# A fused linear-attention and FFN kernel: other warm-up matmuls, other release points for its first loads, and another model of the DMA in its planner

## The chip, the cores and the metric

The kernel runs on one core of one Trainium2 chip. A core has a matrix engine (PE in the profile; its weight loads are shown as PEld), a vector engine (DVE), a scalar engine (ACT), GpSimd (POOL) and a queue engine (SP), each with its own in-order list of instructions; they meet through semaphores. Sixteen DMA engines move data between device memory (HBM) and the on-chip memory. PE writes to eight accumulation banks, which DVE and ACT read.

The metric is the device time of one execution in microseconds. Before the change the median of seven runs is 193.08 us (191.82 to 193.83).

## The reference

```
# q, k, v, f_logit: [4, 8, 768, 48]; moe_w_gate, moe_w_val: [384, 1536]; moe_w_out: [1536, 384]
f = 1 / (1 + exp(-f_logit))
for t in range(768):
    state = f[:, :, t, :, None] * state + outer(k[:, :, t], v[:, :, t])      # per batch and head, 48 x 48
    y[:, :, t] = q[:, :, t] @ state
x = y with heads side by side                                                # [3072, 384]
out = (relu(x @ w_gate) * (x @ w_val)) @ w_out                               # [3072, 384], float32
```

## The kernel before

The sequence is cut into six chunks of 128 tokens. For each chunk c the four batches are taken as two pairs, written c.0 and c.1 in the load order. The recurrence is computed chunk by chunk: cumulative sums of log-forgets by a matmul (L594), exponentials on ACT (L608), q and k scaled by them ("hats", L610), transposes (L642), scores (L667), a mask (L683 on DVE; two of them per pair in chunk 0 by ACT and POOL, L678 and L680), the outputs y (L712, L717) copied to xT (L729), and the state (L692, L564, L568, L570). Chunks 0 and 1 take this form (`attention_pair`); later chunks have a similar one.

The FFN of a chunk follows: twelve steps j of 128 hidden columns. A step has a gate group and a val group of three matmuls each (L922), a relu on ACT (L928) and a product on DVE (L932). Then the output projection (L965) with w_out, a copy (L975) and a store (L979). All FFN groups are chained in the order in which the code creates them (`chain("ffn", ...)`), so a group whose weights are missing holds up every later one. `halves` says, for chunks 0 to 2, how many of the first steps j are done for pair 0 alone and then for pair 1 alone, with 256 columns, before the rest is done for both with 512.

Each of the three weight matrices is loaded in thirds of four steps, cast to bf16 on the way: wg0, wg1, wg2 of w_gate, wv0 to wv2 of w_val, wo0 to wo2 of w_out. POOL issues them (L508), in the order wg0, wv0, wg1, wv1, wg2, wv2, wo0, wo1, wo2. SP issues the loads of f, k, q and v (L487), a whole pair at a time, 384 KB each. The string `first` lists the first loads; `x@y` means that the issuing engine waits for y to have landed before it issues x. The wait stands in the engine's own list, so all that is behind it there waits too: on POOL the elementwise work, on SP the later loads. Later loads of SP wait for a load three places earlier.

The order on every engine comes from a planner (`Plan`): a list scheduler with a fixed duration for each operation takes at each step the operation that can start first, by priority among equals. Its `transfers` works out when each load lands, packet by packet, with the two queues (SP's and POOL's) taking turns; `settle` alternates the two eight times. Only the order that comes out reaches the program, not the planned times.

At the start PE has nothing to do for some microseconds, and fillers are put in: matmuls of zeros into the last bank, whose result nobody reads. The kernel before puts them ahead of any operation planned to start by 15 us: as many matmuls of 512 columns (L1024) as fill 0.6 or 0.9 of the planned gap, after one at the very start (L1015). The zeros are set by DVE (L415).

The prediction speaks of f0.1 (the load of f for pair 1 of chunk 0), v0.0, k0.1, v0.1, q0.1 (named alike), of wg0, wv0, wg1, wv1, and of f1.0, k1.0, q1.0, v1.0, k1.1, wo0 and wo1.

Of the kernel before, what the change touches and what calls it, by code (L numbers as in the profile page):

```python
# [8 lines left out]
BF16 = mybir.dt.bfloat16  # L9
# [33 lines left out]
class Plan:  # L43
# [10 lines left out]
    def add(self, eng, emit, reads=(), writes=(), occ=0.5, lat=0.2, prio=0, opens=(), after=(), follows=()):  # L54
        op = Op(eng, emit, list(reads), list(writes), occ, lat, prio, opens, after, follows)
        op.idx = len(self.ops)
        self.ops.append(op)
        return op
# [128 lines left out]
    def transfers(self):  # L187

        rings = {e: [op for op in self.order[e] if op.parts] for e in ("SP", "POOL")}
        todo, at = {e: [] for e in rings}, {e: 0 for e in rings}  # L190
        issue = {"SP": 0.0}
        held = {e: [] for e in rings}
        sent, owed, t, last = 0, 0, 0.0, None
        pending = None
        sp = rings["SP"]
        queue = {e: [] for e in rings}
        for op in rings["POOL"]:
            queue["POOL"].append([op, op.parts[0], op.start + op.parts[3]])
        nxt = 0

        def feed():
            nonlocal nxt, pending, owed
            while True:
                if pending is not None:
                    if owed - sent > self.depth:
                        return
                    pending.issued = max(t, issue["SP"])
                    issue["SP"] = pending.issued
                    pending = None
                if nxt == len(sp):  # L210
# [12 lines left out]
        while True:  # L223
            feed()
            heads = {e: queue[e][0] for e in queue if queue[e]}
            if not heads:
                break
            can = {e: h for e, h in heads.items() if h[2] <= t}
            if not can:
                times = [h[2] for h in heads.values()]  # L230
                if nxt < len(sp) and pending is None:
                    times.append(max(sp[nxt].ready, issue["SP"]))
                t = max(t + 0.01, min(times))
                continue
            e = next(iter(can)) if len(can) == 1 else ("POOL" if last == "SP" else "SP")
            h = can[e]
            t += h[0].parts[1 if len(can) == 1 else 2] / 1000.0
            last = e
            h[1] -= 1
            if e == "SP":  # L240
                sent += 1
            if h[1] == 0:
                h[0].land = t + (self.tail[0] if e == "POOL" else 0.65 if t < 14.0 else self.tail[1])
                queue[e].pop(0)

    def settle(self, banks, rounds, early):
        self.depth, self.lag, self.tail = 250, 2.4, (1.6, 2.6)
        for i in range(rounds):
            self.schedule(banks)
            if i < rounds - 1:  # L250
                self.transfers()
                for op in self.ops:
                    if op not in early:
                        op.land = op.issued = None
        return self.order
# [47 lines left out]
def bass_hgrn2_outer__then__ffn_reglu_kernel(  # L303
# [10 lines left out]
    twos = (0, 1)  # L314
    pe_hats = {(0, 0), (0, 1), (1, 0), (1, 1)}
    by_pool = {(0, 0, 0, 1), (0, 1, 0, 1)}
    halves = {0: 6, 1: 4, 2: 6}
    x_way = {(c, pr): "tiled" if c < 5 else "xbar" for c in range(6) for pr in range(2)}
    s_twin = {(c, pr) for c in range(6) for pr in range(2)}
    y_twin = {(c, pr) for c in range(2, 5) for pr in range(2)}  # L320
# [1 line left out]
    act_copies, dve_q, single = set(), set(), set()  # L322
    flight = 3
    wsteps = 3
    first = ("f0.0 k0.0 q0.0 v0.0 f0.1 k0.1 v0.1 wg0@f0.1 wv0 wg1 wv1 q0.1 wg2@wv0 wv2 f1.0@wv1 k1.0 q1.0 v1.0 wo0@q1.0 wo1 "
             "k1.1 f1.1 q1.1 v1.1@f1.1 wo2").split()
    B, H, S, D = q.shape
    C = 128
    NC = S // C
# [11 lines left out]
    sb = nc.alloc_sbuf_tensor  # L341
# [40 lines left out]
    mask2 = sb("mask2", [128, 2, 2, 64], BF16)  # L382
    ident = sb("ident", [128, 128], BF16)
    ones = sb("ones", [128, 1], BF16)
    zeros = sb("zeros", [128, 512], BF16)
    banks = [nc.alloc_psum_tensor(f"ps{i}", [128, 512], F32) for i in range(8)]

    pl = Plan({"bc": 2, "bc4": 4, "tp": 2, "s": 4, "y": 2, "kv": 2, "f": 4})
    add = pl.add
    gp, ve, sc, te, sy = nc.gpsimd, nc.vector, nc.scalar, nc.tensor, nc.sync  # L390
# [13 lines left out]
    def pool_t(n):  # L404
        return dict(occ=0.1 + n * 2.2 / 1000.0, lat=0.12)
# [7 lines left out]
    def fill(eng, name, ap, value, cols, prio, key=None):  # L413
        e = engine[eng]
        add(eng, lambda: e.memset(ap, value), [], [key or name], occ=0.07 + cols / (1090.0 if eng == "DVE" else 1020.0), prio=prio)  # L415
# [19 lines left out]
    for t, name, src, sname in ((upto, "upto", tri, "tri"), (below, "below", tris, "tris")):  # L435
        add("DVE", lambda t=t, src=src: ve.tensor_tensor(t[:], src[:], same.ap[:, 0:128], ALU.mult), [same, sname], [name],
            occ=0.25, prio=-19)
    add("DVE", lambda: ve.tensor_copy(pick2[:], same.ap[:, 0:128].rearrange("p (b t) -> p b t", b=2)[:, :, 0]), [same], ["pick2"],
        occ=0.1, prio=-19)
    for i, src, name in ((0, upto, "upto"), (1, below, "below"), (1, upto, "upto")):  # L440
# [3 lines left out]
            src[:, 64:128].unsqueeze(1).to_broadcast([128, len(lo), 64]), ALU.add), [name], [f"mask2_{i}{m}" for m in lo],  # L444
            prio=-9, **pool_t(64 * len(lo)))

    fill("DVE", "zeros", zeros[:], 0.0, 256, -30)
    for i in range(NB):
        fill("DVE", f"bneg{i}", bneg[:, i], 0.0, 512, -28 if i < 1 else 11 if i < 2 else 30)
    for i in range(NH):  # L450
# [47 lines left out]
    def load_w(nm, s, after):  # L498
        if nm == "wo":
            src = bass.AP(tensor=w_out.tensor, offset=s * WJ * 128 * DM,  # L500
                          ap=[[DM, 128], [128 * DM, WJ], [1, DM]])
            dst = wo[:, s * WJ:(s + 1) * WJ, :]
        else:
            src = bass.AP(tensor=wsrc[nm].tensor, offset=s * WJ * 128,
                          ap=[[DFF, 128], [128 * DFF, NK], [1, WJ * 128]])
            dst = (wg if nm == "wg" else wv)[:, :, s * WJ * 128:(s + 1) * WJ * 128]
        last = tails.get("load_w")
        op = add("POOL", lambda: gp.dma_start(dst, src), [], [f"{nm}{s}"], occ=0.8, lat=1.2, prio=50, after=after,  # L508
                 follows=[last] if last else [])
        tails["load_w"] = op  # L510
        dma(op, f"{nm}{s}", 2.45, (32, 62, 80, 2.2) if nm == "wo" else (24, 80, 80, 2.6))
        return op

    loads, done, firsts = [], {}, []
    for item in first:
        item, _, behind = item.partition("@")
        gate = [done[behind]] if behind else []
        if item[0] == "w":
            op = load_w(item[:2], int(item[2:]), gate)
        else:  # L520
            c, b = int(item[1]), int(item[3])
            b0, b1 = (2 * b, 2 * b + 2) if item[2] == "." else (b, b + 1)
            op = load(item[0], c, b0, b1, gate)
# [485 lines left out]
    for item in pend[:-1]:  # L1009
        ffn_out(*item)  # L1010
    ffn_end(NC - 1, B - 1, [(0, 256), (256, DM)])

    WARM = 512
    warm_until = 15.0
    add("PE", lambda: te.matmul(banks[-1][:, 0:WARM], zeros[:, 0:128], zeros[:, 0:WARM]), ["zeros"], ["warm"], occ=0.2,  # L1015
        prio=-30)
    for e in pl.ENGINES:
        pl.free0[e] = 0.8
    spare = banks[-1]
    order = pl.settle([(bk, warm_until if bk is spare else 0.0) for bk in banks], rounds=8, early=set(firsts))  # L1020
    waits = pl.needs()

    def warm():
        return te.matmul(spare[:, 0:WARM], zeros[:, 0:128], zeros[:, 0:WARM], start=True, stop=True, skip_group_check=True)  # L1024

    busy, at, begun = [], pl.free0["PE"], False
    for op in order["PE"]:
        gap, each = op.start - at, 0.44 if at < 4.0 else 0.23
        if begun and op.start <= warm_until:
            for _ in range(int((0.9 if gap > 1.5 else 0.6) * gap / each)):  # L1030
                busy.append((op, warm))
        begun = True
        at = op.start + op.occ
    fillers = {}
    for op, emit in busy:
# [2 lines left out]
    for e in ("PE", "ACT", "DVE", "POOL"):  # L1038
        n = 0
# [75 lines left out]
```

## Time and profile before

| | us |
|---|---|
| median of seven runs (lowest, highest) | 193.08 (191.82, 193.83) |
| the profiled execution | 191.82 |
| its span, first to last instruction of the program | 190.1 |
| PE busy | 181.1 |
| ACT busy | 109.8 |
| DVE busy | 104.8 |
| POOL busy | 75.6 |

Times in the views are microseconds from the start of the span. A timeline row gives start, duration, engine, line, operation, output and inputs, and how many instructions it merges; in brackets stands the idle time ahead of it and what ended that. "POOLq" and "SPq" are the parts of these engines that issue; a DMA row there is the issue of a transfer, not the transfer. The chain of work that ended last is followed back from the last instruction; a DMA in it runs from its issue to its landing, and "issue" is time for which the profile shows no reason.

In the profiled execution f, k, q and v of pair 0 are issued from 0.81 to 2.97 us and those of pair 1 from 4.17 to 7.75. The first weight is issued at 9.41, and the load of f1.0 at 22.13.

### The profile page before, as it was taken

What the parts mean: (1) busy time and instruction counts of PE and PEld (TensorE: products, weight loads), DVE (VectorE), ACT (ScalarE), POOL (GpSimd) and SP (SyncE); (2) the same over time, 40 slices, a digit from 0 to 9 for tenths busy, and PEclk for the clock granted to TensorE, in tenths of its full rate; (3) what the DMA queues carried; (4) which work ended last, traced back from release to release, by engine and by line L of the source; (5) the groups of instructions that cost most, each with busy time, mean ns of one, the idle gap of its engine ahead of it and who ended that gap; (6) DMA issues with size and microseconds to landing.
All of it is one profiled execution on the core that took longest, in us unless ns stands there. A gap on an engine that the chain in (4) does not pass through costs nothing.

```text
span 190.1 us, 5012 instructions
## 1 busy us (share of the span) xinstructions
PE 181.1 (95%) x2061; PEld 107.9 (57%) x2079; DVE 104.8 (55%) x189; ACT 109.8 (58%) x244; POOL 75.6 (40%) x109
## 2 busy tenths in 40 slices
PE   7888799999999999999999999999999999999994
PEld 2456584566685466768545564554555555554564
DVE  7799364994555866518696375625538233343300
ACT  3774459835598486575867739476533533334322
POOL 8497404752376638446375473806300000000000
PEclk9999999999999999999999999999999999999999
DMA  6999999998999999999999999999640310011113
GB/s 158 325 273 204 174 246 282 214 233 166 254 210 211 209 165 211 219 224 222 147 209 196 179 216 213 231 213 226 129 100 19 86 41 32 9 45 41 41 53 112
DMA packets 108854, 32.04 MB, mean 169 GB/s; under 512 B 101792, under 2 KB 108832, under 8 KB 108832
## 3 DMA queue, kind: packets, MB, share of 16 engines
q1 hardware_dynamic: 104848, 28.19, 70.6%
q0 software_dynamic: 3984, 3.54, 11.9%
q8 instruction: 16, 0.26, 0.6%
q14 instruction: 6, 0.05, 0.1%
HBM read 25.95 MB, written 4.72 MB: 161 GB/s over the span
## 4 chain that ended last, share of the span: by engine, by line
PE 82%; DMA 11%; POOL 3%; issue 2%; SPq 1%; ACT 0%; POOLq 0%
PE ps L922 47%; PE ps L965 23%; DMA wo<-in_moe_w_out_dram 4%; DMA wv<-in_moe_w_val_dram 4%; PE ps L852 3%; DMA q_in<-in_q_dram 2%; PE ps L817 2%; POOL hats L610 2%; PE ps L751 1%; PE ps L900 1%; POOL vpad L657 1%; PE ps L945 1%; PE ps L712 1%; SPq L487 1%; PE ps L754 0%
## 5 line engine op out<-in xcount | busy, mean ns | idle before, releaser
L932 DVE TENSOR_TENSOR gT<-relu,ps 128x512 bf16<-128x512 bf16 (+1 forms) x88 | 51.0, 588 | 61.3 <-PE ps L922 38.5
L928 ACT ACTIVATE relu<-ps 128x512 bf16<-128x512 f32 (+1 forms) x88 | 45.6, 522 | 27.9 <-PE ps L922 26.8
L922 PE MATMUL ps<-xT,wv 128*128 128x512 bf16 (+1 forms) x262 | 60.7, 340 | 0.6 <-DMA wv<-in_moe_w_val_dram 0.3
L922 PE MATMUL ps<-xT,wg 128*128 128x512 bf16 (+1 forms) x249 | 57.9, 338 | 0.7 <-issue 0.2
L965 PE MATMUL ps<-wo,gT 128*128 128x384 bf16 x276 | 49.1, 326 | 0.4 <-DMA wo<-in_moe_w_out_dram 0.4
L965 PEld LDWEIGHTS ps<-wo,gT 128*128 128x128 bf16 x276 | 26.2, 98 | 18.7 <-DMA wo<-in_moe_w_out_dram 1.0
L922 PEld LDWEIGHTS ps<-xT,wv 128*128 128x128 bf16 x264 | 25.0, 98 | 19.5 <-DMA wv<-in_moe_w_val_dram 0.4
L922 PEld LDWEIGHTS ps<-xT,wg 128*128 128x128 bf16 x264 | 24.8, 98 | 19.8 <-issue 1.7
L975 ACT ACTIVATE osb<-ps 128x384 f32<-128x384 f32 x23 | 11.2, 494 | 26.5 <-PE ps L965 26.4
L773 POOL TENSOR_TENSOR hats<-k_in,expo 128x384 bf16<-128x384 f32 x16 | 15.8, 998 | 19.0 <-ACT expo L761 15.4
L827 DVE TENSOR_TENSOR ptm<-ps,tri 128x512 bf16<-128x512 f32 x32 | 20.4, 683 | 5.3 <-PE ps L817 5.2
L570 POOL TENSOR_TENSOR st<-ssum,dec 128x384 bf16<-128x384 f32 x16 | 13.1, 832 | 19.9 <-DVE ssum L568 19.9
L777 POOL TENSOR_TENSOR hats<-q_in,expo 128x384 bf16<-128x384 f32 x16 | 15.7, 1000 | 3.7 <-DMA q_in<-in_q_dram 3.7
L568 DVE TENSOR_TENSOR ssum<-ps,st 128x384 f32<-128x384 f32 x16 | 8.4, 552 | 3.7 <-PE ps L900 3.5
L683 DVE TENSOR_TENSOR ptm<-ps,mask 128x512 bf16<-128x512 f32 x14 | 8.7, 680 | 1.7 <-PE ps L667 1.7
L761 ACT ACTIVATE expo<-ps 128x384 f32<-128x384 f32 x16 | 7.9, 491 | 2.8 <-PE ps L754 2.7
L763 ACT ACTIVATE expo<-ps 128x384 f32<-128x384 f32 x16 | 8.0, 500 | 0.0
L807 POOL CAST vpad<-v_in 128x384 bf16<-128x384 f32 x16 | 7.7, 509 | 0.6 <-DMA v_in<-in_v_dram 0.6
L729 ACT ACTIVATE xT<-ps 128x384 bf16<-128x384 f32 x8 | 4.2, 597 | 5.5 <-PE ps L717 5.4
L742 ACT ACTIVATE f_in<-f_in 128x768 f32<-128x768 f32 x8 | 6.7, 842 | 0.8 <-DMA f_in<-in_f_logit_dram 0.8
L744 ACT ACTIVATE bneg<-f_in 128x768 bf16<-128x768 f32 x8 | 6.8, 845 | 0.1
L881 ACT ACTIVATE xT<-ps 128x384 bf16<-128x384 f32 x12 | 5.2, 486 | 2.6 <-PE ps L852 2.6
(85 smaller groups left out, 161.1 us busy)
## 6 DMA issues: line engine op xcount, KB each, us to landing
f_in<-in_f_logit_dram SPq DMA_DIRECT2D x12, 384.0 KB, 5.7
k_in<-in_k_dram SPq DMA_DIRECT2D x12, 384.0 KB, 5.6
q_in<-in_q_dram SPq DMA_DIRECT2D x12, 384.0 KB, 4.9
v_in<-in_v_dram SPq DMA_DIRECT2D x12, 384.0 KB, 5.3
out_dram<-osb SPq DMA_DIRECT2D x23, 192.0 KB, 2.4
wg<-in_moe_w_gate_dram POOLq DMA_DIRECT2D x3, 384.0 KB, 5.6
wv<-in_moe_w_val_dram POOLq DMA_DIRECT2D x3, 384.0 KB, 7.1
wo<-in_moe_w_out_dram POOLq DMA_DIRECT2D x3, 384.0 KB, 8.5
```

The lines of the kernel that those rows point to most:

```text
L568: add("DVE", lambda: ve.tensor_tensor(tmp[:, :], kv.ap[:, 0:HD], s_old[:, :], ALU.add), [kv, f"S{b}_{(c + 1) % 2}"], [key], prio=P + 8, ** ...
L570: add("POOL", lambda: gp.tensor_tensor(t4(s_new), t4(tmp), rate, ALU.mult), [key] + dk, [f"S{b}_{c % 2}"], prio=P + 8, **pool_t(HD))
L683: add("DVE", lambda i=i, j=j, mask=mask: ve.tensor_tensor(ptm[ms[i]][:, j, :, :], s[i][j].ap[:, :].rearrange("p (n t) -> p n t", n=NP), ma ...
L763: add("ACT", lambda: sc.activation(ex[:, 0, :], bc.ap[:, 0:HD], AF.Exp, scale=-1.0), [bc], [f"expq{ei // 2 * 2}_{ei % 2}"], prio=P + 1, ** ...
L773: add("POOL", lambda: gp.tensor_tensor(hk, kin[:, b % 2, :, :], ex[:, 1, :].rearrange("p (h d) -> p h d", h=H), ALU.mult), in_keys("k", c, ...
L777: add(e, lambda: engine[e].tensor_tensor(hq, qin[:, b % 2, :, :], ex[:, 0, :].rearrange("p (h d) -> p h d", h=H), ALU.mult), in_keys("q", ...
L827: add("DVE", lambda mi=mi, j=j, s=s: ve.tensor_tensor(ptm[mi][:, j, :, :], s.ap[:, :].rearrange("p (n t) -> p n t", n=NP), mask, ALU.mult) ...
L922: mm = te.matmul(bank.ap[:, 0:n], wt[:, kt, j * 128:(j + 1) * 128], xT[xi][:, kt, n0:n1], start=(kt == 0), stop=(kt == NK - 1))
L928: add("ACT", lambda: sc.activation(relu[ri][:, 0:n], gate.ap[:, 0:n], AF.Relu), [gate], [f"relu{ri}"], prio=P, **act_t(n))
L932: add("DVE", lambda: ve.tensor_tensor(gT[gi][:, j, n0:n1], relu[ri][:, 0:n], val.ap[:, 0:n], ALU.mult), [val, f"relu{ri}"], [f"gT{gi}_{j}_ ...
L965: mm = te.matmul(o[b].ap[:, 0:DM], gT[gi][:, j, b * C:(b + 1) * C], wo[:, j, :], start=(j == 0), stop=(j == NJ - 1))
L975: add("ACT", lambda b=b, oi=oi: sc.activation(osb[oi][:, :], o[b].ap[:, 0:DM], AF.Copy), [o[b]], [f"osb{oi}"], prio=P, **act_t(DM))
```

## The change

Five things change.

1. The fillers. Instead of a rule there is a list: the first five planned gaps on PE of more than 0.4 us get 18 and 58 matmuls of 64 columns and then 8, 3 and 5 of 128 columns, 92 in all. The opening matmul has 128 columns too. The timeline before shows 16 fillers of 512 columns beside the opening one; a few matmul records can be missing from it.
2. The tile of zeros has 128 columns instead of 512, and its memset is planned as shorter.
3. `halves` of chunk 0 goes from 6 to 8.
4. The string `first`. The order of the loads on SP and of the weights on POOL stays. What changes is what they wait for: f0.1 waits for v0.0 (before: for nothing), wv0 for wg0 (nothing), wg1 for v0.0 (nothing), k1.0 for f1.0 (nothing), q1.0 for q0.1 (nothing), wo0 for k1.1 (q1.0), wo1 for k1.1 (nothing), v1.1 for nothing (f1.1). wg0 waits for f0.1, wg2 for wv0 and f1.0 for wv1 in both.
5. The planner's transfers. At seven listed times all transfers stop for 0.55 us; for that, the time from the last packet to the landing is 0.7 us instead of 1.6 (weights) and 2.6 us (loads after 14 us). This alters the planned landings, and by them the order on the engines.

```diff
@@ transfers
+        fetch = list(self.fetch)
...
+            if fetch and fetch[0] <= t:
+                fetch.pop(0)
+                t += self.stall
+                last = None
+                continue
@@ settle
-        self.depth, self.lag, self.tail = 250, 2.4, (1.6, 2.6)
+        self.depth, self.lag, self.tail = 250, 2.4, (0.7, 0.7)
+        self.stall = 0.55
+        self.fetch = [8.5, 16.8, 25.3, 30.0, 43.6, 48.0, 53.5]
@@ the kernel
-    halves = {0: 6, 1: 4, 2: 6}
+    halves = {0: 8, 1: 4, 2: 6}
...
-    first = ("f0.0 k0.0 q0.0 v0.0 f0.1 k0.1 v0.1 wg0@f0.1 wv0 wg1 wv1 q0.1 wg2@wv0 wv2 f1.0@wv1 k1.0 q1.0 v1.0 wo0@q1.0 wo1 "
-             "k1.1 f1.1 q1.1 v1.1@f1.1 wo2").split()
+    first = ("f0.0 k0.0 q0.0 v0.0 f0.1@v0.0 wg0@f0.1 k0.1 wv0@wg0 v0.1 wg1@v0.0 wv1 wg2@wv0 q0.1 f1.0@wv1 wv2 k1.0@f1.0 q1.0@q0.1 "
+             "v1.0 k1.1 f1.1 wo0@k1.1 wo1@k1.1 q1.1 v1.1 wo2").split()
...
-    zeros = sb("zeros", [128, 512], BF16)
+    zeros = sb("zeros", [128, 128], BF16)
...
-    fill("DVE", "zeros", zeros[:], 0.0, 256, -30)
+    fill("DVE", "zeros", zeros[:], 0.0, 64, -30)
...
-    add("PE", lambda: te.matmul(banks[-1][:, 0:WARM], zeros[:, 0:128], zeros[:, 0:WARM]), ["zeros"], ["warm"], occ=0.2,
-        prio=-30)
+    add("PE", lambda: te.matmul(banks[-1][:, 0:128], zeros[:, :], zeros[:, :]), ["zeros"], ["warm"], occ=0.1, prio=-30)
...
-    busy, at, begun = [], pl.free0["PE"], False
+    def warm(n):
+        return te.matmul(spare[:, 0:n], zeros[:, :], zeros[:, 0:n], start=True, stop=True, skip_group_check=True)
+
+    busy, at, short = [], None, [(64, 18), (64, 58), (128, 8), (128, 3), (128, 5)]
     for op in order["PE"]:
-        gap, each = op.start - at, 0.44 if at < 4.0 else 0.23
-        if begun and op.start <= warm_until:
-            for _ in range(int((0.9 if gap > 1.5 else 0.6) * gap / each)):
-                busy.append((op, warm))
-        begun = True
+        gap = op.start - at if at is not None else 0.0
+        if short and gap > 0.4:
+            n, many = short.pop(0)
+            busy += [(op, lambda n=n: warm(n))] * many
         at = op.start + op.occ
```

More of the change, by code (lines that the diff above doesn't have):

```diff
@@ L1011, in bass_hgrn2_outer__then__ffn_reglu_kernel @@
     ffn_end(NC - 1, B - 1, [(0, 256), (256, DM)])
-    WARM = 512
-    warm_until = 15.0
-    add("PE", lambda: te.matmul(banks[-1][:, 0:WARM], zeros[:, 0:128], zeros[:, 0:WARM]), ["zeros"], ["warm"], occ=0.2,
-        prio=-30)
+    add("PE", lambda: te.matmul(banks[-1][:, 0:128], zeros[:, :], zeros[:, :]), ["zeros"], ["warm"], occ=0.1, prio=-30)
     for e in pl.ENGINES:
@@ L1019, in bass_hgrn2_outer__then__ffn_reglu_kernel @@
     spare = banks[-1]
-    order = pl.settle([(bk, warm_until if bk is spare else 0.0) for bk in banks], rounds=8, early=set(firsts))
+    order = pl.settle([(bk, 15.0 if bk is spare else 0.0) for bk in banks], rounds=8, early=set(firsts))
     waits = pl.needs()
-    def warm():
-        return te.matmul(spare[:, 0:WARM], zeros[:, 0:128], zeros[:, 0:WARM], start=True, stop=True, skip_group_check=True)
-    busy, at, begun = [], pl.free0["PE"], False
+    def warm(n):
+        return te.matmul(spare[:, 0:n], zeros[:, :], zeros[:, 0:n], start=True, stop=True, skip_group_check=True)
+    busy, at, short = [], None, [(64, 18), (64, 58), (128, 8), (128, 3), (128, 5)]
     for op in order["PE"]:
-        gap, each = op.start - at, 0.44 if at < 4.0 else 0.23
-        if begun and op.start <= warm_until:
-            for _ in range(int((0.9 if gap > 1.5 else 0.6) * gap / each)):
-                busy.append((op, warm))
-        begun = True
+        gap = op.start - at if at is not None else 0.0
+        if short and gap > 0.4:
+            n, many = short.pop(0)
+            busy += [(op, lambda n=n: warm(n))] * many
         at = op.start + op.occ
```

## The prediction

> **What bounds the kernel now.** I read the page's busy times first, then busy times by stretch, the chain in order of time, and the timelines of POOL, SP's queue and PE.
>
> ```profile
> PE 181.1 (95%) x2061; PEld 107.9 (57%) x2079; DVE 104.8 (55%) x189; ACT 109.8 (58%) x244; POOL 75.6 (40%) x109
> ```
>
> PE is the busy engine, but an average hides the front, and fillers count as busy. The second view cuts the span where PE becomes dense (columns: stretch, length, each engine's busy time, then clock and DMA):
>
> ```profile
> core 0: us, PE busy (x) PEld busy (x) DVE busy (x) ACT busy (x) POOL busy (x), PEclk, DMA share, GB/s
> 15.50:22.46 6.96, 4.74 (x137) 3.47 (x134) 5.17 (x11) 2.13 (x5) 4.57 (x6) 1.00 1.21 192
> 22.46:50.00 27.54, 26.88 (x356) 17.49 (x357) 19.81 (x34) 17.59 (x38) 9.49 (x12) 1.00 1.09 231
> 50.00:100.00 50.00, 49.74 (x675) 32.79 (x681) 29.83 (x58) 36.37 (x95) 30.13 (x37) 1.00 1.15 203
> 100.00:150.00 50.00, 49.37 (x496) 27.19 (x493) 25.96 (x42) 29.39 (x60) 19.04 (x25) 1.00 0.82 169
> 150.00:188.00 38.00, 37.61 (x212) 20.24 (x211) 11.20 (x17) 14.12 (x26) 0.00 (x0) 1.00 0.12 45
> ```
>
> From 22.46 to 188 PE idles 0.66 + 0.26 + 0.63 + 0.39 = 1.94 us. So the end is the start of the dense part plus the work left then, and the front decides. The chain there:
>
> ```profile
> 10.35 7.11 DMA wv<-in_moe_w_val_dram
> 17.46 0.05 issue
> 17.50 2.47 PE ps L922 x21
> ...
> 20.91 1.39 issue
> 22.31 0.22 PE ps L717
> 22.52 5.35 PE ps L922 x48
> ```
>
> The first projections wait for the first third of w_val (wv0, landed 17.46). Then comes a 1.39 us stop in the y matmuls that nothing in the program explains ("issue"). POOL and SP's queue issue the transfers:
>
> ```profile
> 9.41 0.94 POOL L508 DMA_DIRECT2D wg<-in_moe_w_gate_dram  x1
> 10.35 0.78 POOL L508 DMA_DIRECT2D wv<-in_moe_w_val_dram  x1
> 11.12 0.77 POOL L508 DMA_DIRECT2D wg<-in_moe_w_gate_dram  x1
> ...
> 17.75 0.80 POOL L508 DMA_DIRECT2D wg<-in_moe_w_gate_dram  x1 [1.20 <-DMA wv<-in_moe_w_val_dram]
> ```
>
> ```profile
> 2.97 1.16 SPq L487 DMA_DIRECT2D v_in<-in_v_dram  x1
> 4.17 1.15 SPq L487 DMA_DIRECT2D f_in<-in_f_logit_dram  x1
> ...
> 22.13 0.37 SPq L487 DMA_DIRECT2D f_in<-in_f_logit_dram  x1
> ```
>
> Three weights go out back to back and only the third gate load waits, for wv0 (17.46, issue 17.75). f0.1 goes out right behind v0.0. f1.0 shows what a gate does: wv1 was issued at 14.88 and took 7.2 us to land, 22.1, and f1.0 leaves at 22.13. On PE:
>
> ```profile
> 17.50 0.50 PE L922 MATMUL ps<-xT,wv 128*128 128x256 bf16 x3 [0.27 <-DMA wv<-in_moe_w_val_dram]
> 17.84 0.49 PE L922 MATMUL ps<-xT,wg 128*128 128x256 bf16 x3
> ```
>
> Groups of three start 0.33 us apart. By 22.46 there are eight of them; the ninth, the gate of j=4, starts there.
>
> [...] The page has 16 packets, 0.26 MB, on queue 8: 16 KiB each. [...]
>
> **The change part by part.**
>
> *Fillers.* The wide ones (16 recorded beside the opening one) go, 92 short ones come. [...] the trace has 427 ns for 512 columns. So 64 columns cost an estimated 53 ns: 18 x 53 = 0.96 us in the gap from about 1.2 to 2.22, and 58 x 53 = 3.1 us from 2.44 to 5.5, before the cumulative sums at 5.95. Eight of 128 columns follow, 0.45 us warm, in a wait that held six wide ones (1.46 us); the last eight take about as much. All lie in waits for data: 0 on the path. If the cover were gone, the gap after 5.5 is 0.4 us. The clock is at 1.00 in every stretch above[...]. The instruction count grows by about 150[...]. Bounds -1.4 to +1.4; I take 0[...].
>
> *Zeros.* 512 to 128 columns: 0.27 us of DVE become about 0.1. The DVE later waits 0.51 us for ACT at 7.13, which hides it: 0.
>
> *Halves 6 to 8.* Two steps j go from 512 to 256 columns: 12 matmuls of 0.216 us become 24 of 0.109, +0.02 us. ACT and DVE get two instructions more each, about 0.4 us, under 10 and 7.7 us of idle from 22.46 to 50. Its effect is order: pair 0 now has j=0 to 7 before pair 1.
>
> *f0.1 waits for v0.0.* v0.0 lands at 2.97 + 4.8 = 7.8. With the queue drained, f0.1 takes f0.0's 3.3 us: 11.1, against 8.99. Behind it on SP stand k0.1, v0.1 and q0.1, 1.2 us apart: 12.3, 13.5, 14.7. All of pair 1 comes at least 2.1 us later; its y matmuls, 19.90 now, start at 22 to 23.
>
> *wg0 waits for f0.1.* That wait is there already, but POOL passed it at 9.41, behind the v copies. Now 11.1; its 5.3 us from issue to landing gives 16.4 (14.7 now).
>
> *wv0 waits for wg0.* New. Issued at 16.4, with POOL blocked from its turn; the next POOL work (pair 1's products) is due then or is planned ahead of it. Another 5.3 us: wv0 lands at 21.7, against 17.46. The DMA engines stand still meanwhile.
>
> *wg1, wv1.* Their gates cost nothing, v0.0 being long there. They leave right behind wv0. Landings now are 17.46, 19.4 and 22.1, so 1.95 and 2.7 apart: wg1 23.7, wv1 26.4. If both are 1.95 apart, wv1 is there at 25.6.
>
> *What PE makes of it.* The projections go in one written order: with halves 8, four steps of pair 0 on the first thirds (8 x 0.33 = 2.6 us, 21.7 to 24.4; or from about 23 if pair 1's y matmuls go first), the gate of j=4, then its val group, which needs wv1: 26.4. This state, nine groups and the attention of chunk 0 done, is reached at 22.46 + 0.33 = 22.8 now. **Delay 26.4 - 22.8 = 3.6 us**; low end 2.8. The old stop of 1.39 us is inside 22.8 already and can't be won twice.
>
> *Chunk 1 and wo.* f1.0 still waits for wv1: 26.4 + its 5.9 = 32.3. k1.0 now waits for f1.0: +3.3 = 35.6; q1.0, v1.0 and k1.1 at 36.8, 38.0, 39.2. wo0 and wo1 wait for k1.1 instead of q1.0: issue 39.2, and with wo0's own 6.8 us landing at 46.0 (44.5 with 5.3). PE takes up wo0 at 39.35 now, so it wants it at 43.0: short by 1.5 to 3.0. But pair 1's q and v of chunk 1 now come ahead of wo (about 42 instead of 44), so its transposes and state (1.07 + 0.51 us), and more scores and y, fill the gap. I take 1.0 us of idle, bounds 0 and 3. Against it, the present 0.45 us wait for wo2 can go: -0.3.
>
> *Planner.* Fetch stalls and shorter tails change only planned times; they reorder the in-order engines. With 1.94 us of idle after 22.46, no order can win more than about 1 us there; a loss up to 1.5 is possible. I take 0.
>
> Sum: 3.6 + 1.0 - 0.3 = **+4.3 us**. The profiled execution took 191.82 (span 190.1, 1.7 around it), so 196.1 on that footing. It is the fastest of the seven runs; on their median, 193.08, it is 197.4, and I put down 197.2.
>
> **Rivals.** *Front delay alone* (17%): weights closer together, wo fully covered: +2.8 - 0.5, about 195.4. For it: the 1.95 spacing is measured. Against: every wait behind wv1 also moves. *Delay and more* (8%): POOL's blocking, a stop in pair 1's y matmuls or a half-speed clock come on top, about 200. For it: 22 us of thin PE work; against: the waits overlap. *Faster* (8%), on the other side: [...] wv1 then lands before PE wants it and 1.39 us plus some idle are won: about 191.3. The point of decision is wv1 landing before 22.8. Against it, three issue-to-landing times in series (3.3 + 5.3 + 5.3 from 7.8) already reach 21.7 for wv0, when two more weights have to follow. *No effect* (5%): the gates are passed late anyway and planned order pays the rest back; it needs wv1 near 23.5.
>
> **Numbers.** The likeliest case has 62%, with a range of its own of 195.5 to 199.5. Slower by over 0.5% (1 us, about what this measurement can tell): 62 + 17 + 8 = 87%; within 0.5%: 5%; faster 8%. The range 194.0 to 200.5 takes in the low end of the front delay and most of the costly case, and leaves out the faster one and no change.
>
> **What would show it.** Right: f0.1 issued just after 7.8 and landing near 11; a pause of some 2 us in the loads; wv0 issued only when wg0 is there and landing at 21 to 23; PE waiting for wv at the first val group and perhaps again at j=4; PE dense from about 26; k1.0 issued at f1.0's landing. Wrong if wv0 lands before 19, if PE's first val group starts before 20, or if PE idles clearly less than now between 15 and 30.

## The result and the profile after

| | before | after |
|---|---|---|
| median, us (lowest, highest; executions) | 193.55 (191.09, 196.44; 64) | 198.2 (193.23, 201.54; 27) |
| profiled execution, us (its span) | 191.82 (190.1) | 199.14 (197.4) |
| granted clock in the profiled execution | 1.00 | 0.974 |

The ratio is 1.009 (95% interval 1.0055 to 1.0125), some 1.7 us; here and in the table of the experiments it leaves out executions more than 1.5% above the fastest of their kernel, which are most of those of the changed kernel. That is why the medians stand further apart, at 198.2 / 193.55 = 1.024. The changed kernel's executions, 28 with one that the median doesn't count, fall into steps by their granted clock: two at 1.00 (193.2 and 193.7), nine at 0.99 (eight about 195, one at 199.3), sixteen at 0.98 (196.5 to 201.5, median 198.5) and the profiled one at 0.974. Of 124 executions of the kernel before that stood beside the experiments, 121 were at 0.999 or 1.00 and three at 0.991. The slower clock is therefore part of the change's effect. One stretch of 3.41 us at half speed takes 0.5 x 3.41 / 197.4 = 0.9% off the mean, so the steps fit none, one, two and three such stretches; the profiled executions show one at 0.991 (only_releases), two at 0.983 (all_but_planner) and three at 0.974 (after).

The span grew by 7.3 us. First the busy times on the page of after, then its stretches, cut where the clock or PE's activity changes (stretch, length, busy time of PE, PEld, DVE, ACT and POOL, granted clock, DMA share, GB/s):

```profile
PE 184.9 (94%) x2149; PEld 114.1 (58%) x2166; DVE 105.0 (53%) x191; ACT 110.2 (56%) x246; POOL 76.4 (39%) x109
```

```profile
14.16:17.57 3.41, 1.77 (x40) 1.15 (x39) 2.99 (x6) 1.44 (x3) 2.70 (x4) 1.00 1.24 207
17.57:20.98 3.41, 2.82 (x18) 2.23 (x19) 0.89 (x2) 0.38 (x1) 2.42 (x3) 0.50 1.24 204
20.98:46.80 25.82, 24.76 (x451) 17.62 (x451) 21.38 (x41) 16.53 (x39) 11.95 (x14) 1.00 1.12 223
46.80:49.29 2.49, 0.00 (x1) 0.01 (x1) 1.75 (x3) 1.69 (x2) 0.07 (x1) 0.80 0.87 173
49.29:55.12 5.83, 5.83 (x97) 3.02 (x98) 0.00 (x0) 2.94 (x10) 4.51 (x6) 0.50 0.52 106
```

PE is no less busy than before; some of that time is work at half speed. At clock 0.50 eight output matmuls take 2.72 us, 340 ns each (L973 at 50.17 below); before, at clock 1.00, sixteen took 2.77, 173 ns each (L965 at 47.11 below). The second row holds 2.82 us of PE work at clock 0.50; half of it lost, by these numbers, is an estimated 1.4. The last holds 5.83: 2.9 lost. Between them PE stands still for 2.5. Together that is 6.8 of the 7.3 us. Two other differences nearly cancel: the stop of 1.39 us before the last y matmul is gone, and PE waits for wv0 1.38 us instead of 0.27. After 55.12 the clock is full again.

The chain of work that ended last leads to the place (start, length, what; rows of "issue" of at most 0.05 us between these are left out):

```profile
28.89 6.40 DMA f_in<-in_f_logit_dram
35.31 12.18 DMA f_in<-in_f_logit_dram
47.52 0.85 ACT f_in L750
48.39 0.85 ACT bneg L752
49.29 0.50 PE ps L759
```

The two loads are f1.1 and f2.0, the forget gates of chunk 2. f2.0 takes 12.18 us from issue to landing; then come two steps on ACT and the cumulative sums of chunk 2 on PE (L759). Before, no wait for f2.0 stood in the chain. Yet f2.0 was slow there too: it was issued at 34.81, and the view of it alone gives

```profile
DMA to landing us min/median/max: 10.8/10.8/10.8
```

But PE came to the sums of chunk 2 later, behind sixteen output matmuls, and had no wait:

```profile
47.11 2.77 PE L965 MATMUL ps<-wo,gT 128*128 128x384 bf16 x16
49.72 0.33 PE L751 MATMUL ps<-bneg,tri 128*128 128x384 bf16 x1
```

In after PE comes to them at 46.8 (49.29 - 2.51). So what is new is the early place of the sums rather than a slow load. POOL's issues, SP's issues and PE in after:

```profile
9.71 0.94 POOL L516 DMA_DIRECT2D wg<-in_moe_w_gate_dram  x1
10.64 0.78 POOL L516 DMA_DIRECT2D wv<-in_moe_w_val_dram  x1
...
35.60 2.29 POOL L516 DMA_DIRECT2D wo<-in_moe_w_out_dram  x3
```

```profile
2.98 1.40 SPq L495 DMA_DIRECT2D v_in<-in_v_dram  x1
4.42 1.15 SPq L495 DMA_DIRECT2D f_in<-in_f_logit_dram  x1
...
35.31 0.37 SPq L495 DMA_DIRECT2D f_in<-in_f_logit_dram  x1
```

```profile
18.16 0.82 PE L930 MATMUL ps<-xT,wv 128*128 128x256 bf16 x3 [1.38 <-DMA wv<-in_moe_w_val_dram]
...
45.95 0.82 PE L973 MATMUL ps<-wo,gT 128*128 128x384 bf16 x4
49.29 0.50 PE L759 MATMUL ps<-bneg,tri 128*128 128x384 bf16 x1 [2.51 <-ACT bneg L752]
...
50.17 2.72 PE L973 MATMUL ps<-wo,gT 128*128 128x384 bf16 x8
```

f0.1 is issued at 4.42, right behind v0.0, which landed only at 8.13; wv0 goes out right behind wg0. Neither waits for anything, so the waits that I priced are not there. What is new sits in the order on PE. The first val group stands ahead of pair 1's second transposes and waits for wv0. The sums of chunk 2 stand among the output projections and wait for f2.0, which went out 0.29 us ahead of a burst of three wo transfers. The output groups behind the sums (L973, 50.17) had weights by then: wo0 had landed at 42.48 and wo1 at 45.67.

**Why the waits are missing.** `link` reads

```
for d in op.after:
    deps[d] = "raw"
for d in op.follows:
    deps[d] = "order"
```

`follows` holds the load just before on the same queue. A release that names that very load (f0.1@v0.0, wv0@wg0, k1.0@f1.0) is entered as "raw" and then overwritten by "order", and `needs` skips "order". So these three entries of the list under "The change" are no waits in the program. Against the kernel before, the new string makes two differences that can hold or free a load: wo0 waits for k1.1 instead of q1.0, and v1.1 no longer waits for f1.1. The others name loads that have long landed (in after q0.1 at 15.86, with q1.0 issued at 23.19; v0.0 at 8.13, with wg1 issued at 11.42) or, for wo1, the load that wo0 has waited for.

### The profile page after: what moved, and what is told of

It reads as the page before. It is cut to its first block, busy times and chain, and to the rows that moved or that the text cites. A ratio compares the mean times of both kernels' runs of the same rounds, so it can differ in the third digit from the quotient of the medians.

```text
span 197.4 us, 5198 instructions
## 1 busy us (share of the span) xinstructions
PE 184.9 (94%) x2149; PEld 114.1 (58%) x2166; DVE 105.0 (53%) x191; ACT 110.2 (56%) x246; POOL 76.4 (39%) x109
## 4 chain that ended last, share of the span: by engine, by line
PE 70%; DMA 16%; SPq 4%; POOL 3%; ACT 2%; issue 2%; DVE 2%; POOLq 0%
PE ps L930 37%; PE ps L973 23%; DMA f_in<-in_f_logit_dram 9%; DMA wv<-in_moe_w_val_dram 4%; SPq L495 4%; DMA q_in<-in_q_dram 2%; PE ps L860 2%; PE ps L825 2%; PE ps L759 1%; PE ps L908 1%; PE ps L953 1%; POOL vpad L665 1%; POOL wg L516 1%; DVE gT L940 1%; DVE ptm L835 1%
## 5 line engine op out<-in xcount | busy, mean ns | idle before, releaser
L940 DVE TENSOR_TENSOR gT<-relu,ps 128x512 bf16<-128x512 bf16 (+1 forms) x90 | 51.2, 578 | 71.0 <-PE ps L930 38.2
L930 PE MATMUL ps<-xT,wv 128*128 128x512 bf16 (+1 forms) x269 | 61.9, 339 | 1.7 <-DMA wv<-in_moe_w_val_dram 1.4
L973 PE MATMUL ps<-wo,gT 128*128 128x384 bf16 x276 | 51.5, 334 | 0.0
L930 PEld LDWEIGHTS ps<-xT,wv 128*128 128x128 bf16 x270 | 25.6, 99 | 20.4 <-DMA wv<-in_moe_w_val_dram 1.7
L973 PEld LDWEIGHTS ps<-wo,gT 128*128 128x128 bf16 x276 | 26.5, 99 | 18.7 <-issue 1.6
L930 PEld LDWEIGHTS ps<-xT,wg 128*128 128x128 bf16 x270 | 25.5, 99 | 18.6 <-ACT xT L737 1.0
L781 POOL TENSOR_TENSOR hats<-k_in,expo 128x384 bf16<-128x384 f32 x16 | 15.9, 999 | 27.4 <-ACT expo L769 19.0
L889 ACT ACTIVATE xT<-ps 128x384 bf16<-128x384 f32 x12 | 5.3, 487 | 4.9 <-PE ps L860 4.9
L618 POOL TENSOR_TENSOR hats<-k_in,expo 128x384 bf16<-128x384 f32 x4 | 4.2, 1072 | 8.2 <-ACT expo L616 8.2
L759 PE MATMUL ps<-bneg,tri 128*128 128x384 bf16 x16 | 4.9, 346 | 2.5 <-ACT bneg L752 2.5
## 6 DMA issues: line engine op xcount, KB each, us to landing
out_dram<-osb SPq DMA_DIRECT2D x23, 192.0 KB, 2.3
```

What stands on the lines that cost most here:

```text
L781: add("POOL", lambda: gp.tensor_tensor(hk, kin[:, b % 2, :, :], ex[:, 1, :].rearrange("p (h d) -> p h d", h=H), ALU.mult), in_keys("k", c, ...
L930: mm = te.matmul(bank.ap[:, 0:n], wt[:, kt, j * 128:(j + 1) * 128], xT[xi][:, kt, n0:n1], start=(kt == 0), stop=(kt == NK - 1))
L940: add("DVE", lambda: ve.tensor_tensor(gT[gi][:, j, n0:n1], relu[ri][:, 0:n], val.ap[:, 0:n], ALU.mult), [val, f"relu{ri}"], [f"gT{gi}_{j}_ ...
L973: mm = te.matmul(o[b].ap[:, 0:DM], gT[gi][:, j, b * C:(b + 1) * C], wo[:, j, :], start=(j == 0), stop=(j == NJ - 1))
```

## The experiments

Ratios are against the kernel before on the same chip, with 95% intervals.

| kernel | median us (executions) | ratio |
|---|---|---|
| only_halves | 191.58 (12) | 0.9987 (0.9962 to 1.0012) |
| only_fillers | 193.02 (20) | 0.999 (0.996 to 1.0021) |
| only_releases | 194.16 (17) | 1.0068 (1.0041 to 1.0096) |
| only_planner | 194.43 (20) | 1.0089 (1.0064 to 1.0113) |
| all_but_releases | 195.42 (4) | 1.0128 (1.0066 to 1.0191) |
| all_but_planner | 199.31 (5) | 1.0084 (1.0051 to 1.0116) |
| all_but_fillers | 193.69 (12) | 1.0047 (1.0012 to 1.0082) |
| gates_hold | 202.13 (4) | 1.055 (1.0507 to 1.0593) |
| f2_ahead | 194.45 (6) | 1.0134 (1.0103 to 1.0166) |
| sums_later | 194.28 (6) | 1.009 (1.0055 to 1.0126) |
| kept_warm | 194.25 (4) | 1.0131 (1.0094 to 1.0168) |
| f2_ahead_wide | 193.19 (6) | 1.0068 (1.0045 to 1.009) |
| sums_later_wide | 192.62 (17) | 1.0039 (1.0015 to 1.0064) |
| sums_later_wide_transposes | 193.55 (21) | 1.0059 (1.0036 to 1.0081) |

The parts do not add up in these ratios: only_releases and only_planner alone make 0.7% and 0.9%, the whole change 0.9%.

### One part alone

**only_fillers**: the short fillers and the small tile of zeros, in the kernel before.

```diff
-    zeros = sb("zeros", [128, 512], BF16)
+    zeros = sb("zeros", [128, 128], BF16)
...
-    busy, at, begun = [], pl.free0["PE"], False
+    busy, at, short = [], None, [(64, 18), (64, 58), (128, 8), (128, 3), (128, 5)]
...
```

> The kernel before with the 92 short fillers (and the small tile of zeros) alone; the planned order stays that of before. Theory 'fillers' (150 more PE instructions bring an instruction block's fetch from 14.1 us to about 8.9 us, into the front loads[...]): k0.1 lands near 11.8 instead of 10.2, q0.1 near 15.9 instead of 12.6, wg0 near 16.2 instead of 14.7, and the time is 1 to 2 us above before. Theories 'placing' and 'planned landings': no change, within 0.7 us of before, granted clock 1.00 from about 6 us on.

No difference in time. In the trace, though, q0.1 takes 6.3 us from issue to landing, against 4.9 before, and PE waits 0.83 us for wv0 (0.27 before).

**only_halves**:

```diff
-    halves = {0: 6, 1: 4, 2: 6}
+    halves = {0: 8, 1: 4, 2: 6}
```

> The kernel before with halves of 8 instead of 6 in chunk 0 alone. All theories: within 0.5% of before (ratio 0.996 to 1.005), PE busy the same to 0.1 us, two more relus and products.

No difference.

**only_releases**: the new string alone.

```diff
-    first = ("f0.0 k0.0 q0.0 v0.0 f0.1 k0.1 v0.1 wg0@f0.1 wv0 wg1 wv1 q0.1 wg2@wv0 wv2 f1.0@wv1 k1.0 q1.0 v1.0 wo0@q1.0 wo1 "
-             "k1.1 f1.1 q1.1 v1.1@f1.1 wo2").split()
+    first = ("f0.0 k0.0 q0.0 v0.0 f0.1@v0.0 wg0@f0.1 k0.1 wv0@wg0 v0.1 wg1@v0.0 wv1 wg2@wv0 q0.1 f1.0@wv1 wv2 k1.0@f1.0 q1.0@q0.1 "
+             "v1.0 k1.1 f1.1 wo0@k1.1 wo1@k1.1 q1.1 v1.1 wo2").split()
```

> The kernel before with the new string of loads alone; by the code only three of its differences are waits at all: wo0 for k1.1 instead of q1.0, v1.1 no longer for f1.1, q1.0 for the long landed q0.1. Theory 'placing' (the planner now puts chunk 2's cumulative sums ahead of output projections, PE waits there for f2.0, and the idle stretch halves the PE clock): PE waits 2 us or more before a chunk 2 sum between 40 and 50 us, at least one half-clock window of 3.4 us after it, time 3 to 6 us above before. Theories 'fillers' and 'planned landings': within 0.7 us of before. The prediction's theory (gates that hold loads) would want wv0 near 21.7: not expected any more.

Slower by 0.7%, without delayed weights: no load waits for v0.0 or wg0. The sums of chunk 2 are at 45.09 on PE (49.72 before). They need not wait in the profiled execution, where f2.0 went out 1.67 us ahead of wo0 and took 4.05 us. One of the 17 executions had clock 0.983, and it took 200.56. What costs the 0.7% was not isolated. In the trace PE waits 1.20 us for DVE's masked scores at 42.33, as it does in all_but_planner at 40.12 and not before; the clock also fell once, from 18.38 to 21.80.

**only_planner**: the stalls and the short tails alone.

```diff
-        self.depth, self.lag, self.tail = 250, 2.4, (1.6, 2.6)
+        self.depth, self.lag, self.tail = 250, 2.4, (0.7, 0.7)
+        self.stall = 0.55
+        self.fetch = [8.5, 16.8, 25.3, 30.0, 43.6, 48.0, 53.5]
...
```

> The kernel before with the new transfer model of the planner alone (0.55 us stops, tails of 0.7 us). The order on PE has the first val group, which needs wv0, ahead of pair 1's second transposes and scores. Theory 'planned landings': PE waits for wv0 0.5 to 1.5 us ahead of work that was ready, pair 1's y matmuls move from 19.9 to 22 or later, a half-clock window can follow; time 1 to 3 us above before. Theories 'fillers' and 'placing': within 0.7 us of before.

Slower by 0.9%. On PE:

```profile
17.52 0.50 PE L930 MATMUL ps<-xT,wv 128*128 128x256 bf16 x3 [1.44 <-DMA wv<-in_moe_w_val_dram]
```

wv0 lands where it did; the order now asks for it before pair 1's second transposes, and pair 1's y matmuls start at 22.23 instead of 19.90. The sums of chunk 2 stay late, at 50.71. That this place of the val group is what costs the 0.9% is argued from the trace; the last of the combinations below does not bear it out.

### One part left out

**all_but_releases**, the change with the old string:

```diff
-             "v1.0 k1.1 f1.1 wo0@k1.1 wo1@k1.1 q1.1 v1.1 wo2").split()
...
+             "k1.1 f1.1 q1.1 v1.1@f1.1 wo2").split()
```

> The changed kernel with the old string of loads. Chunk 2's sums stand late among the output projections again. Theory 'placing': no wait over 0.5 us between 40 and 52 us and no half-clock window there; time 3 to 5 us under the changed kernel's median of 198.2, so 193 to 195. Theory 'planned landings' or 'fillers': the front stays as in the changed kernel, with wv0 landing near 18.1 and a half-clock window at 17 to 21 in some executions, worth 1.2 to 1.7 us; if these two are all of it the time stays near 198.

Four executions from 194.27 to 195.94, none below clock 0.991. The sums of chunk 2 are back at 51.18.

**all_but_planner**, the change with the old model of transfers:

```diff
-        self.depth, self.lag, self.tail = 250, 2.4, (0.7, 0.7)
...
+        self.depth, self.lag, self.tail = 250, 2.4, (1.6, 2.6)
```

> The changed kernel with the old transfer model in the planner. The front's order is that of before; chunk 2's sums stand even earlier than in the change, ahead of the first output projection. Theory 'planned landings make both': the wait for wv0 ahead of ready work goes, and the time comes to 193 to 194. Theory 'placing by the releases': PE still waits for f2.0 or for chunk 1's products between 40 and 50 us, time 1 to 2 us above before, as with the releases alone (ratio 1.007).

Three of five executions had clock 0.98 and took 199.3 to 200.0, so the new model of transfers isn't needed for the long wait. PE in the profiled one:

```profile
47.12 0.41 PE L751 MATMUL ps<-bneg,tri 128*128 128x384 bf16 x1 [4.13 <-ACT bneg L744]
```

Taken with the kernels above, the string brings the early sums, whichever model plans: PE reaches them at 43.0 (47.12 - 4.13) here, 45.1 in only_releases and 46.8 in after, but at 51.2 in all_but_releases, 50.7 in only_planner and 49.7 before. f2.0 is released by f1.1 with both strings, so this goes by the planner: the list scheduler places the sums by the landing that it works out. That link is read from the code.

**all_but_fillers**, the change with the wide fillers:

```diff
...
-    busy, at, short = [], None, [(64, 18), (64, 58), (128, 8), (128, 3), (128, 5)]
+    busy, at, begun = [], pl.free0["PE"], False
...
```

> The changed kernel with the old wide fillers and tile of zeros, the planned order being that of the change. Theory 'fillers bring instruction blocks forward into the loads': k0.1, q0.1, wg0 land as before (10.2, 12.6, 14.7) and the time falls by 1 to 2 us at the same clock. Theory 'fillers do nothing' (their part alone gave a ratio of 0.999): the same mixture as the changed kernel, most executions with two half-clock windows, median 197 to 198.5.

Better than the whole change, and in steps: five executions at 1.00 (about 192.0), four at 0.991 (193.6 to 196.1), three at 0.98 (195.4 to 198.5). The profiled one has the long wait:

```profile
48.14 0.50 PE L759 MATMUL ps<-bneg,tri 128*128 128x384 bf16 x1 [3.96 <-ACT bneg L752]
```

So the wait doesn't come from the fillers, but the kernel loses less without them.

### The waits that I had priced, made real

**gates_hold**: the change, with the two loops of `link` exchanged, so that a named release wins over the order.

```diff
-            for d in op.after:
-                deps[d] = "raw"
             for d in op.follows:
                 deps[d] = "order"
+            for d in op.after:
+                deps[d] = "raw"
```

> The changed kernel with the two loops that build an operation's dependencies exchanged, so that a release point that names the load just before it on its own queue is waited for (f0.1 for v0.0, wv0 for wg0, k1.0 for f1.0). This is the program that the prediction costed. By its sum f0.1 leaves at about 8.0 and lands at 11.1, wv0 leaves when wg0 is there (16.4) and lands at 21.7, wv1 at 26.4; 4.3 us above before at full clock (about 197), more if the idle stretch of PE before wv0 halves the clock: 1 to 2 us. If the gates cost nothing even when they hold, the time stays at the changed kernel's 193.5 to 198.5.

5.5% slower. SP's issues, POOL's and PE:

```profile
7.67 0.37 SPq L495 DMA_DIRECT2D f_in<-in_f_logit_dram  x1
...
28.60 0.37 SPq L495 DMA_DIRECT2D f_in<-in_f_logit_dram  x1
33.57 0.37 SPq L495 DMA_DIRECT2D k_in<-in_k_dram  x1
```

```profile
12.62 0.94 POOL L516 DMA_DIRECT2D wg<-in_moe_w_gate_dram  x1
18.64 0.80 POOL L516 DMA_DIRECT2D wv<-in_moe_w_val_dram  x1 [1.71 <-DMA wg<-in_moe_w_gate_dram]
```

```profile
22.23 1.01 PE L720 MATMUL ps<-ptm,vpad 64*32 64x128 bf16 x64 [2.30 <-POOL ptm L688]
28.63 0.50 PE L930 MATMUL ps<-xT,wv 128*128 128x256 bf16 x3 [1.20 <-DMA wv<-in_moe_w_val_dram]
```

Here are the pictures of the prediction: f0.1 issued at 7.67 behind v0.0 and landing at 11.05 (11.1 forecast), wv0 held for wg0 and landing at 23.41 (21.7), PE waiting 1.20 us for wv1, which lands at 28.58 (26.4), k1.0 held for f1.0. Most of the two microseconds between comes from wg0, issued at 12.62 and not at 11.1, because POOL's elementwise work stands ahead of it. Ahead of its first val group PE waits not for wv0 but 2.30 us for POOL's masked scores (L688), which stand behind the held weights in POOL's list. The median is 10.3 us above that of before, not 4.3. The rest of the change is in this kernel too: it stands at 202.13 / 191.86 = 1.054, the changed kernel at 1.024.

### The wait for f2.0

**f2_ahead**: wo0 waits for q1.1, one load later, so that f2.0 gets further ahead of it.

```diff
-             "v1.0 k1.1 f1.1 wo0@k1.1 wo1@k1.1 q1.1 v1.1 wo2").split()
+             "v1.0 k1.1 f1.1 q1.1 wo0@q1.1 wo1 v1.1 wo2").split()
```

> The changed kernel with wo0 waiting for q1.1 instead of k1.1 (wo1 for nothing). f2.0 waits for f1.1, which lands 1.2 us before q1.1, so f2.0 is now always issued more than 1 us ahead of wo0. In the traces so far f2.0 took 4.0 us to land where it led wo0 by 1.1 and 1.7 us, and 10.2 to 12.6 us where it led by 0.3 us or came after it. Theory 'race' (the executions near 198 are those in which f2.0 gets among the three wo transfers, PE waits for it ahead of the output projections and drops to half clock): f2.0 lands within 5 us, no execution above 196, no clock at 0.983 or below, median 193 to 195. Theory 'placing without the race' (chunk 2's sums stand too early whatever f2.0 does): the wait and the executions near 198 stay.

f2.0 now goes out 1.56 us ahead of wo0. f2.0 alone, first in after, then in f2_ahead:

```profile
DMA to landing us min/median/max: 12.2/12.2/12.2
```

```profile
DMA to landing us min/median/max: 4.4/4.4/4.4
```

PE no longer waits for it, though the sums stand at 42.92 here, earlier still than in after. Six executions lie between 193.8 and 195.9, one of them at a clock below 0.99 (of the changed kernel 17 of 28); the changed kernel's usual 198.5 does not occur. The ratio in the table, however, is no better than that of the whole change: what this removes is the upper steps.

**sums_later**: loads as in the change; on PE alone, the first two sums of chunk 2 change places with the two operations behind them, which belong to the output projection; positions are renumbered.

```diff
+    pe = order["PE"]
+    sums = [op for op in pe if "ones" in op.reads][:2]
+    at = pe.index(sums[1])
+    later = pe[at + 1:at + 3]
+    pe[at - 1:at + 3] = later + sums
...
```

> The changed kernel with chunk 2's first two cumulative sums moved on PE alone behind the two output projection groups that followed them (eight matmuls, 1.3 us); all else, the race of f2.0 with wo0 too, as it was. Theory 'race and head of line': in executions that lose the race PE waits 1.3 us less, and the half-clock windows of 6.8 us become rare or shorter, so these executions come down from 198.5 to 194.5 to 197; the others stay at 193.5 to 195. Theory 'late data, order no matter': 198.5 stays, because later work waits for the same f2.0.

```profile
43.88 2.12 PE L973 MATMUL ps<-wo,gT 128*128 128x384 bf16 x12
...
45.84 0.33 PE L759 MATMUL ps<-bneg,tri 128*128 128x384 bf16 x1
```

f2.0 was slow here too (8.9 us), and PE has no wait: it does twelve output matmuls first. The sums take 0.33 us at full clock (0.50 in after). Six executions, 192.41 to 196.49, median 194.28, none below clock 0.991. In medians against before on the same chip, the whole change stands at 1.024 and this at 194.28 / 192.09 = 1.011 (f2_ahead: 1.012). A reordering on PE alone takes off about half of the loss, so that half is the wait in front of the output groups, with the slow clock behind it.

**kept_warm**: the change with 56 more matmuls of zeros, ahead of the operations that come just before the first gate group, the first val group and the sums of chunk 2, so that PE would be busy through the waits. Nobody reads their results.

```diff
+        for key, many in (("wg0", 8), ("wv0", 18), ("ones", 30)):
...
+                    te.matmul(ahead[op][0][:, 384:512], zeros[:, :], zeros[:, :], start=True, stop=True, skip_group_check=True)
```

> The changed kernel with 56 more fillers of 128 columns, put ahead of the three PE operations that stand before its waits (8 before chunk 0's second state update, 18 before the first gate group, 30 before the output projection group that precedes chunk 2's sums). Waits and loads stay. Theory 'clock' (most of the loss is the PE at half clock after idle stretches): granted clock 1.00 in nearly all executions, no execution near 198, median 193.5 to 195. Theory 'waits alone': executions with a long wait for f2.0 stay at 197 to 199, whatever the clock.

All four executions were at clock 1.00 (two of 28 of the changed kernel), so with the 56 matmuls no half-speed stretch came. But in the profiled one f2.0 had landed at 37.48, and the 30 matmuls (some 1.7 us) covered no wait. How much of the loss is clock and how much is waiting stays open.

### Combinations

**f2_ahead_wide** and **sums_later_wide** are the two kernels above with the wide fillers; **sums_later_wide_transposes** also moves pair 1's second transposes ahead of the first val group on PE, with the waits worked out in that order.

```diff
-    zeros = sb("zeros", [128, 128], BF16)
+    zeros = sb("zeros", [128, 512], BF16)
```

> As the run with wo0 waiting for q1.1, with the old wide fillers and tile of zeros: planner, releases but this one, and halves are the change's. It is the candidate to beat both kernels. All-but-fillers at full clock stood at the kernel before's time (192.0 against 191.9). Theory 'race': no execution above 195, median 191.5 to 193, ratio 0.997 to 1.005. Theory 'planned landings cost by themselves' (the planner's part alone gave 1.009 at full clock, with the 1.4 us wait for wv0 ahead of ready work): ratio 1.005 to 1.012.

> As the run with chunk 2's sums moved behind two output projection groups, with the old wide fillers. Two of the three suspected costs of the change are undone at once: the instruction block that comes early into the loads, and the place of the sums. If the costs add, the median falls from 194.3 by 1.0 to 1.5 us (as from 194.45 to 193.19 in the pair with f2.0 ahead), to a ratio of 0.998 to 1.004; if the wide fillers win nothing beyond undoing the long wait, it stays at 1.007 to 1.010.

```diff
+    val = next(op for op in pe if "wv0" in op.reads)
+    v_at = pe.index(val)
+    second = next(op for op in pe[v_at:] if "ident" in op.reads)
+    t_at = pe.index(second)
+    pe[v_at:t_at + 1] = [second] + pe[v_at:t_at]
...
```

> As that, and pair 1's second group of transposes stands ahead of chunk 0's first val group on PE, so that it can run in the 1.4 us wait for wv0. The third suspected cost, the planner's order in the front, is partly undone. If it is that order which leaves the planner's part alone at 1.009, the time falls by a further 0.3 to 1.0 us, with pair 1's y matmuls earlier than 22.2 us by about 0.6; if the wait for wv0 is what ends last anyway, no difference (within 0.3 us).

With wide fillers f2_ahead falls by 1.3 us (194.45 to 193.19, same chip). sums_later goes from 1.011 to 192.62 / 191.73 = 1.005, again some 1.3 us. So, undone in this sequence, the wait for f2.0 accounts for about 1.3 of the 2.4% between the medians and the short fillers for 0.7, and 0.4 to 0.5 remain. The split goes by the sequence: with the fillers undone first (all_but_fillers, 193.69 / 191.86 = 1.010) they account for some 1.4, and the place of the sums for 0.5. These are medians of few executions on several chips, and by what path the short fillers cost time was not found. Moving the transposes gains nothing (1.0059 against 1.0039): PE then stands 1.32 us for the hats that they read, instead of 1.55 us for wv0, and f2.0, issued 0.22 us behind wo0 in the profiled execution, took 11.7 us and held up even the later sums by 1.66 us. None of these is faster than the kernel before. What keeps sums_later_wide 0.4% above it was not split further; PE's wait for wv0 is there in its trace.

## Why the prediction was wrong in its steps

The forecast was 197.2 with a range of 194.0 to 200.5, and slower; the median is 198.2. That it lies in the range is a coincidence: the mechanism behind it did not occur. By the ratio of 1.009 the change costs 1.7 us, less than half of the 4.3 of the sum.

**f0.1 waits for v0.0; wv0 waits for wg0; k1.0 waits for f1.0.** These are the steps that failed, and with them "what PE makes of it" (+3.6). I read the notation `x@y` and not the code that turns it into waits. No such wait is issued, so in after wv0 landed at 18.11 and not at 21.7. The prediction's own test for being wrong, wv0 landing before 19 or PE's first val group starting before 20, was met (18.11 and 18.16). What came in place of that delay is a new order on PE: it reached the sums of chunk 2 early, waited 2.5 us for f2.0 and then ran at half clock. Even as a price for real gates the sum fell short, 4.3 against 10.3 for gates_hold, of which some 5.7 us (1.054 less 1.024) come with the gates: I had POOL free at wg0's turn and took its blocking for a rival's extra.

**Chunk 1 and wo: +1.0, bounds 0 and 3.** I followed wo0 to PE and saw it late. It came early enough: landed at 42.48, first used at 43.64. The load that mattered beside its burst was f2.0, which I had not listed.

**Planner: 0, loss up to 1.5.** The model of transfers alone costs 0.9%, 1.7 us (1.2 to 2.2), near the bound and not the 0 that I took. The trace suggests the val group placed ahead of the transposes, but moving them back won nothing, so the cause stays open. The argument that PE idles only 1.94 us after 22.46 bounds what an order can win, and said nothing of what a misplaced wait can lose. The largest piece, the early sums, is an order too, but the string brings it.

**Fillers: 0, bounds -1.4 to +1.4.** Right alone (ratio 0.999). In company with the new orders they cost some 1.3 us where the wait for f2.0 is undone, and some 2.8 us where it is not (1.0240 less 1.0095, of 192). The stop of 1.39 us in the y matmuls is gone from after, but from only_planner and only_releases too, which keep the wide fillers: what made it was not shown.

**Zeros and halves: 0 and +0.02.** Right for halves; the zeros were run only with the fillers.

**A half-speed clock** stood in a rival with 8%, tied to thin PE work in the front. It became the main part: 4.3 of the 7.3 us in the profiled execution, which had three slow stretches where most have two, and 2.9 of it near 50 us where I held PE for dense.

## What to carry to other kernels

Follow a planned release into the code that emits waits before pricing it; a label in a schedule may emit nothing. Look for operations that are planned close to a load's landing: in after one such wait stopped PE for 2.51 us, with output groups behind it whose weights had landed, and the slow clock afterwards cost an estimated 2.9 more. When a change shifts transfers, list every load issued near a burst, not only those whose gates are edited: f2.0 took 4.4 us to land when issued 1.56 us ahead of the wo transfers (f2_ahead) and 12.2 us at 0.29 ahead (after).

## What the runs showed of the hardware

**One load close to a burst.** The time of f2.0 from issue to landing goes with how far it is issued ahead of wo0, the first of three transfers from the other queue:

| issued ahead of wo0 by, us | landing after, us |
|---|---|
| 1.67, 1.56, 1.48, 1.08 | 4.05, 4.4, 4.45, 4.0 |
| 0.33 | 5.35 |
| 0.29, 0.28 | 12.2, 10.6 |
| -0.12, -0.22, -0.35, -0.66 | 8.9, 11.7, 12.6, 12.1 |
| -4.16 to -5.04 (five kernels, the one before among them) | 9.9 to 12.1 |

Between 0.33 and 0.29 us ahead it goes from 5.35 to 12.2. Each figure is one execution, and the kernels differ in other ways too; why it is a step was not tested.

**When the clock drops.** Two stretches of after, each of 3.41 us, ahead of a drop and in it:

```profile
44.88:48.29 3.41, 1.63 (x36) 0.86 (x36) 3.26 (x7) 0.77 (x1) 0.83 (x1) 1.00 1.03 171
48.29:51.70 3.41, 2.41 (x15) 1.25 (x16) 0.26 (x1) 2.66 (x8) 1.09 (x2) 0.50 1.10 223
```

The slow stretches of after last 3.41 us (17.57 to 20.98) and 6.83 us (48.29 to 55.12), and the two drops are 48.29 - 17.57 = 30.72 us apart, 9 x 3.413. In all_but_planner the slow stretch at 47.25 also lasts 6.83 us. Ahead of the two drops of after PE was busy for 1.63 us here and for 1.77 us ahead of 17.57, about half of each 3.41 us. The clock also fell behind stretches of this length with 1.75 us (f2_ahead, 40.74 to 44.15) and 1.88 us (only_releases, 14.97 to 18.38); in gates_hold it did not behind one with 1.84 us (46.22 to 49.63, seven such lengths after its drop at 22.32). The busy time alone does not fix the border. If the clock changes only in steps of 3.41 us, as these lengths suggest, the same waits can fall into one step or be split over two, and executions would differ by that. This is an estimate from the lengths above; the place of the steps was not varied.

**Instruction packets among loads.** The page of after has 17 packets, 0.28 MB, on queue 8, which it calls "instruction": some 16 KB each. With short fillers the first of them starts at 8.9 us in after, with wide ones at 14.1 us before; it takes 0.95 us in both. q0.1 takes 6.0 to 7.8 us from issue to landing in four kernels with short fillers (sums_later and kept_warm 6.0, only_fillers 6.3, after 7.8) and 4.9 us in three with wide ones (before, all_but_fillers, f2_ahead_wide). That the packet is what delays it was not shown: no run moved the packet without the fillers.
